# The first step of a fused FFT attention and MLP kernel: a constant matrix loaded and placed later, a load spread over more rows, the last input piece halved

## The chip, the core and the metric

The kernel runs on one core of a Trainium2 chip. A core has a matrix engine (TensorE; the profile calls it PE, and its weight loads PEld), a vector engine (DVE), a scalar engine (ACT), GpSimd (POOL) and a sync engine (SP), and 16 DMA engines. SP and POOL issue the DMAs; what SP issues appears in the profile as queue q1 (hardware), what POOL issues as q0 (software). The metric is the device time of one execution in microseconds (us); less is better.

## The reference

The input x has 8 batches of 3008 tokens with 256 features. Each batch goes through a real FFT along the tokens, a complex linear layer, a soft threshold and an inverse FFT; the result goes through an MLP with a squared ReLU.

```python
X = np.fft.rfft(x, axis=1)
Yr = Xr @ w_r - Xi @ w_i + b_r
Yi = Xr @ w_i + Xi @ w_r + b_i
Y = sign(Y) * max(abs(Y) - 0.01, 0)      # real and imaginary part alike
y = np.fft.irfft(Y, n=3008, axis=1)      # then, with 256 -> 2048 -> 256:
out = (s * max(y @ w_in, 0)**2 + b) @ w_out
```

## The kernel before, in words

3008 tokens are written as 94 x 32 (N1 = 94, N2 = 32), and the FFT is done with matrices. A first matrix A_t (94 x 96) acts on the 94, a forward matrix (the table F_t, and for the imaginary part the tables F_2) acts on the 32, then comes the linear layer, and an inverse matrix T_t and a last matrix C_t bring the result back. The MLP follows: `first_mm` (L1125), a ReLU and a square (L1154 to L1165), and `second_mms` and `seven_mms` (L1241, L1340).

**Two parts.** Batch 0 is done ahead of everything else in `first_batch` (L550). There the framework orders the instructions of each engine from their dependencies; `issue_after(ins)` places what stands under it behind `ins` on the same engine. From there to the end the order is written out by hand (`manual_schedule`, L1494): a table TURNS says which engine takes which copy and when, and each tile of the MLP is interleaved with the FFT work of the next batch. All matrix multiplications go through one helper, so they all carry the line L225; they are told apart by their tiles.

**The first step of batch 0** is the loop in L553 to L589. It has eight groups of four of the 32 columns of x. The x rows come in four tiles of eight columns (`emit_load_x`, L357), each in two DMAs from POOL that also turn f32 into f16: eight pieces of 188 KB, 94 rows each. A group does four matmuls with x and A_t for each half of the features (dc = 0 and 1), each of 96 columns. The results leave PSUM through `evac` (L233), which gives dc = 0 to ACT (L237) and dc = 1 to DVE (L239), into the tile `ut`. Behind each group `keep_awake(5)` adds five matmuls of ones with ones that compute nothing that is used; 40 of them stand ahead of the first group.

**The second stage** starts with `mix` (L602: `ut` times the weights W_t; a bias is added on DVE in L620, the other half is copied by ACT in L617), which needs all 32 columns of `ut`. `fwd_dft` (L630) multiplies by F_t and F_2 and adds a bias through a selector matrix (`sel_t`, a part of the tile `small`), `inv_dft` (L656) multiplies by T_t, and `turn` and `last_dft` bring the data into the form that the MLP reads. There are twelve such steps (ec, u), with u from 0 to 5; step u uses the entries 4u to 4u+3 of the forward matrix.

**The forward matrix** comes for the first 12 of 24 entries in a compact form F_c, which has to be placed into F_t and, with one sign changed, into F_2[0]. `place_f` (L482) does this for a range of entries: one copy on DVE and one on ACT for F_t (L487), and two pairs on DVE for F_2 (L488, L491). The other 12 entries come ready made (F_t[:, H:] and F_2[1]).

**The loads on SP's queue**, in the order in which SP issues them: A_t, the weights w_r and w_i (256 KB each), four bias rows, F_c entries 0 to 3 (64 KB), the selector (32 KB), F_c entries 4 to 11 (128 KB), and then T_t, F_t[:, H:], F_2[1] and T_t[:, H:] with 384 KB each. Two of these are held back by a tiny `memset` on DVE that writes into the target first: F_c entries 4 to 11 until the fourth group has left PSUM (L586), T_t and the rest until the sixth (L580). `place_w` (L478), two casts of the weights on ACT, stands behind the fourth group. Entries 0 to 3 are placed behind the sixth group, entries 4 to 11 behind the first `mix`. When F_t[:, H:] has landed, a copy on POOL (L591) lets the x rows of batch 1 and the MLP weights w_in and w_out be loaded.

Of the kernel before, what the change touches and what calls it, by code (L numbers as in the profile page):

```python
# [15 lines left out]
P = 128  # L16
N1 = 94
# [71 lines left out]
def _tables(n):  # L89

    k1 = np.array([[1 + 2 * p, 2 + 2 * p] for p in range(NPAIR - 1)] + [[0, N1 // 2]])
    n1 = np.arange(N1)
    n2 = np.arange(N2)
    k2 = np.arange(N2)
    first = np.zeros((N1, 96))
    last = np.zeros((96, 96))
    fwd = np.zeros((P, NPAIR, 64))  # L100
    inv = np.zeros((P, NPAIR, 64))
    for p in range(NPAIR):
        for a in range(2):
            c = k1[p, a]
            real = c in (0, N1 // 2)
            th1 = 2 * np.pi * ((n1 * c) % N1) / N1
            kap = 4 * p + 2 * a
            first[:, kap] = np.cos(th1)
            last[kap, :N1] = np.cos(th1)
            if not real:  # L110
                first[:, kap + 1] = -np.sin(th1)
                last[kap + 1, :N1] = -np.sin(th1)
            k = c + N1 * k2
            flip = k > n // 2
            drop = flip if real else np.zeros_like(flip)
            th = 2 * np.pi * (np.outer(n2, k) % n) / n
            sg = np.where(flip, -1.0, 1.0)
            keep = np.where(drop, 0.0, 1.0)
            edge = (k == 0) | (k == n // 2)

            r0 = a * 64
            cr, ci = a * 32, 64 + a * 32
            fwd[r0 : r0 + 32, p, 0:32] = np.cos(th) * keep
            fwd[r0 : r0 + 32, p, 32:64] = -np.sin(th) * sg * keep
            if not real:
                fwd[r0 + 32 : r0 + 64, p, 0:32] = np.sin(th)
                fwd[r0 + 32 : r0 + 64, p, 32:64] = np.cos(th) * sg

            w = np.where(edge, 1.0, 2.0) * keep * VSCALE
            wi = np.where(edge, 0.0, w) * sg  # L130
            inv[cr : cr + 32, p, 0:32] = (np.cos(th) * w).T
            inv[ci : ci + 32, p, 0:32] = (-np.sin(th) * wi).T
            if not real:
                inv[cr : cr + 32, p, 32:64] = (np.sin(th) * w).T
                inv[ci : ci + 32, p, 32:64] = (np.cos(th) * wi).T
    return first, fwd, inv, last
# [13 lines left out]
def kernel(  # L150
# [21 lines left out]
    HW = N2 // 2  # L172

    first, fwd, inv, last = _tables(N)
    last = last / (N * VSCALE)
    A_d = nc.inline_tensor(first.astype(np.float16), name="dft_first").ap()

# [49 lines left out]
    def work(engine, us):  # L227
        load[engine] += us
# [128 lines left out]
    def emit_load_x(b, chunks=range(N2 // XCH)):  # L357
        xv = x[b].rearrange("(n1 n2) d -> n1 (n2 d)", n2=N2)
        for c in chunks:
            if b < 2 and c == N2 // XCH - 1:  # L360
                t = x2pool.tile([P, XCH * D], F16, name="x2", tag="x2")
            else:
                t = xpool.tile([P, XCH * D], F16, name="x16", tag="x16")
            parts = 2 if b == 0 else 1
            w = XCH * D // parts
            for i in range(parts):
                nc.gpsimd.dma_start(
                    out=t[0:N1, i * w : (i + 1) * w],
                    in_=xv[:, c * XCH * D + i * w : c * XCH * D + (i + 1) * w],
                )  # L370
            x16[(b, c)] = t

# [9 lines left out]


    A_t = cpool.tile([P, 96], F16, name="A_t")
    nc.sync.dma_start(out=A_t[0:N1, :], in_=A_d)
    emit_load_x(0)
    W_t = cpool.tile([P, DC, 2, D], F16, name="W_t")
    w_st = []
    for w in (w_r, w_i):
        st = rpool.tile([P, DC, D], F32, name="w_st", tag="rt")  # L390
        nc.sync.dma_start(out=st, in_=w.rearrange("(c p) e -> p c e", p=P))
        w_st.append(st)

    b_g = tpool.tile([P, 2, D], F32, name="b_g", tag="tail")
# [26 lines left out]
    def load_f_c(q):  # L421
        nc.sync.dma_start(out=F_c[:, q].rearrange("p q r k -> p q (r k)"), in_=F_d[:, q])

    load_f_c(slice(0, 4))

    def emit_load_forward():
        load_f_c(slice(4, H))
        nc.sync.dma_start(out=sel_t, in_=S_d)

    def emit_load_inverse():  # L430
        nc.sync.dma_start(out=T_t[:, 0:H], in_=t_d[:, 0:H])
        nc.sync.dma_start(out=F_t[:, H:], in_=f_d)
        nc.sync.dma_start(out=F_2[1], in_=f_2_d)
        t_load = nc.sync.dma_start(out=T_t[:, H:], in_=t_d[:, H:])
        with tc.issue_after(t_load.ins):
            nc.sync.dma_start(out=eye_t, in_=E_d)
            nc.sync.dma_start(out=C_t, in_=C_d)
            for i, bv in enumerate((b_r, b_i)):
                nc.sync.dma_start(out=b_st[:, i], in_=bv.unsqueeze(0).to_broadcast([P, D]))
            nc.sync.dma_start(out=s_bc, in_=moe_s.unsqueeze(0).to_broadcast([P, 1]))  # L440
            nc.sync.dma_start(out=bb_bc, in_=moe_b.unsqueeze(0).to_broadcast([P, 1]))
# [33 lines left out]
    def blocks(t):  # L475
        return t.rearrange("p q (r a k) -> p q r a k", r=2, a=2)
# [2 lines left out]
        for i in range(2):  # L479
            nc.scalar.copy(out=W_t[:, :, i], in_=w_st[i])  # L480

    def place_f(q):  # L482

        for a in range(2):
            r = slice(64 * a, 64 * a + 64)
            copy = nc.scalar.copy if a else nc.vector.tensor_copy
            copy(out=blocks(F_t)[r, q, :, a], in_=F_c[r, q])  # L487
            nc.vector.tensor_scalar_mul(  # L488
                out=blocks(F_2[0])[r, q, 0, a], in0=F_c[r, q, 1], scalar1=-1.0
            )  # L490
            nc.vector.tensor_copy(out=blocks(F_2[0])[r, q, 1, a], in_=F_c[r, q, 0])  # L491


    w_sum = small[:, 2:4]
# [55 lines left out]
    def first_batch():  # L550
        ut = ypool.tile([P, DC, 96, N2], F16, name="ut", tag="yt")
        last_dve = last_act = None
        last_pe = keep_awake(40)  # L553
        for g in range(N2 // 4):
            c, h = divmod(g, 2)
            for dc in range(DC):
                ps = one_bank() if dc else mix_bank()
                with tc.issue_after(last_pe.ins):
                    for j in range(4):
                        lo = (4 * h + j) * D + dc * P  # L560
                        mm = matmul(
                            ps[:, j * 96 : j * 96 + 96],
                            x16[(0, c)][0:N1, lo : lo + P], A_t[0:N1, :],
                            start=True, stop=True,
                        )
                last_pe = mm
                on_dve, on_act = evac(
                    ut[:, dc, :, 4 * g : 4 * g + 4],
                    ps[:, 0:384].rearrange("p (n k) -> p k n", k=96), 384,
                )  # L570
                last_dve = on_dve or last_dve
                last_act = on_act or last_act
            with tc.issue_after(last_pe.ins):
                last_pe = keep_awake(5)
            if h == 0:
                continue
            if c == 2:
                with tc.issue_after(last_dve.ins):
                    for t in (T_t[:, 0:H], F_t[:, H:], F_2[1], T_t[:, H:]):
                        nc.vector.memset(t[0:1, 0, 0:1], 0.0)  # L580
                emit_load_inverse()
                with tc.issue_after(last_dve.ins), tc.issue_after(last_act.ins):
                    place_f(slice(0, 4))
            if c == 1:
                with tc.issue_after(last_dve.ins):
                    nc.vector.memset(F_c[0:1, 4, 0, 0:1], 0.0)  # L586
                emit_load_forward()
                with tc.issue_after(last_act.ins):
                    place_w()  # L589

# [131 lines left out]
        steps = [(ec, u) for ec in range(DC) for u in range(U)]  # L722
        for i in range(2 * U + 2):
            if i < 2 * U:
                left = mix(*steps[i])
            if i == 0:
                with tc.issue_after(left[0].ins), tc.issue_after(left[1].ins):
                    place_f(slice(4, H))
            if 0 <= i - 1 < 2 * U:
                fwd_dft(*steps[i - 1])  # L730
            if 0 <= i - 2 < 2 * U:
                inv_dft(*steps[i - 2])
            k = i - U - 2
            if 0 <= k < 4:
                turn(0, 8 * k)
                turn(0, 8 * k + 4)
            for n in {1: (0, 4), 2: (8, 12), 4: (16, 20, 24, 28)}.get(k, ()):
                last_dft(0, n)
            if i >= 2 * U:
                some(3)  # L740
            if i == 9:

                gate = nc.gpsimd.tensor_copy(out=low[0:1, 0, 0:1], in_=vt[0:1, 1, 0, 0:1])
                with tc.issue_after(gate.ins):
                    make_w_g()
                    make_bounds()
                    sum_w_out()
# [838 lines left out]
```

## Time and profile before

| what | value |
|---|---|
| time, median of 3 runs | 810.1 us (809.83 to 810.39) |
| the profiled execution's own time | 810.04 us |
| its span, first to last instruction | 808.2 us |
| granted TensorE clock over the span | 1.000 |
| chain that ended last, share of PE | 93% |
| first group of the first step starts | 5.39 us |
| first `mix` starts | 14.54 us |
| first matmul of the MLP | 44.85 us |

The page gives the busy time of each engine over the span. The chain that ended last is followed back from the last instruction; its shares say which engine the end waited for. The timeline lists instructions in order of time, with equal neighbours merged: start, busy time, engine, line, what is written and read, and how often. In brackets stands how long the engine stood idle before the first of them and what ended that. A row of waits reads: the waiting engine and what it writes, what it waited for, the total in us, how many times, the longest. A row of the table of stages gives the stretch, its length, then the busy time and count for each of PE, PEld, DVE, ACT and POOL, the granted clock, the share of the DMA engines and GB/s. A row of a DMA queue gives its packets, its MB, and the time of its packets as a share of 16 engines.

### The profile page before, as it was taken

The page shows a single profiled execution, that of the slowest core. Times are in us where ns is not written, and L with a number is a line of the kernel's source. Part 1 is how long each engine was busy: PE and PEld are TensorE (multiplying, and loading weights), DVE is VectorE, ACT ScalarE, POOL GpSimd, SP SyncE. Part 2 cuts the span into 40 slices and gives each one's busy share as a digit, 9 for nine tenths or more (in the row PEclk, how much of TensorE's full clock was granted, in tenths as well). Part 3 has the DMA queues.
Part 4 walks back from the last instruction along what each step waited for, and adds up shares of the span by engine and source line. Part 5 has one row for each costly group of instructions (what it writes and reads, how often), then busy time and mean ns, then how long its engine had stood idle before and what let it go on. Part 6 is the DMA issues. An engine that isn't in the chain of part 4 may idle for free.

```text
span 808.2 us, 22126 instructions
## 1 busy us (share of the span) xinstructions
PE 799.2 (99%) x9006; PEld 613.1 (76%) x9006; DVE 758.9 (94%) x1342; ACT 749.4 (93%) x932; POOL 107.0 (13%) x151
## 2 busy tenths in 40 slices
PE   8999999999999999999999999999999999999998
PEld 7857767777777977788777886778867788777876
DVE  5899999999999999999999999999999999999895
ACT  5989999999999999999999999999999999998984
POOL 4540001110110101111011210012000100000000
PEclk9999999999999999999999999999999999999999
DMA  8983387555774658665686666666556434732213
GB/s 205 190 194 78 95 237 184 102 136 153 208 151 86 153 139 226 145 124 113 169 200 145 135 145 161 152 154 136 137 164 177 108 80 119 183 67 58 62 41 79
DMA packets 120766, 112.89 MB, mean 140 GB/s; under 512 B 9933, under 2 KB 98129, under 8 KB 120665
## 3 DMA queue, kind: packets, MB, share of 16 engines
q1 hardware_dynamic: 102409, 80.55, 36.0%
q0 software_dynamic: 18256, 30.94, 23.2%
q8 instruction: 70, 1.15, 0.6%
q14 instruction: 31, 0.25, 0.1%
HBM read 53.52 MB, written 46.66 MB: 124 GB/s over the span
## 4 chain that ended last, share of the span: by engine, by line
PE 93%; DMA 0%; ACT 0%; DVE 0%; issue 0%; DVEq 0%; ACTq 0%
PE psh L225 40%; PE psa L225 34%; PE psf L225 19%; DMA out_dram<-ost 0%; DVE ost L1278 0%; ACT rt L1154 0%; ACT u L288 0%; DVEq L1278 0%; ACTq L1154 0%
## 5 line engine op out<-in xcount | busy, mean ns | idle before, releaser
L225 PE MATMUL psh<-yt,w_in 128*128 128x512 f16 (+3 forms) x1792 | 444.5, 343 | 0.2 <-ACT rt L1154 0.2
L225 PEld LDWEIGHTS <-gt 128*128 128x128 f16 x4400 | 306.7, 98 | 141.7 <-DVE gt L1325 2.4
L1154 ACT ACTIVATE rt<-psh 128x1024 f32<-128x1024 f32 x339 | 346.9, 1025 | 23.7 <-PE psh L225 21.5
L1163 ACT ACTIVATE gt<-rt 128x1024 f16<-128x1024 f32 x277 | 289.6, 1059 | 3.1 <-DVE rt L1156 0.7
L225 PE MATMUL psa<-w_out_t,gt 128*128 128x128 f16 (+1 forms) x2208 | 199.6, 224 | 0.0
L225 PEld LDWEIGHTS <-w_in 128*128 128x128 f16 x1824 | 152.0, 98 | 15.8 <-issue 1.4
L225 PE MATMUL psa<-T_s,gt 128*128 128x128 f16 x1824 | 144.3, 219 | 0.0
L1317 POOL DMA_DIRECT2D gt<-gt x63 | 54.8, 870 | 650.0 <-DVE s L1325 194.3
L1165 DVE TENSOR_TENSOR gt<-rt 128x1024 f16<-128x1024 f32 x99 | 120.0, 1216 | 2.4 <-ACT rt L1154 2.1
L1390 DVE SCALAR_TENSOR_TENSOR ost<-psa,s_bc,bias_bc 128x256 f32<-128x256 f32 x152 | 72.6, 478 | 6.7 <-PE psa L225 5.7
L1325 DVE TENSOR_TENSOR gt<-gt 128x1024 f16<-128x1024 f16 x109 | 74.4, 682 | 0.7
L1390 DVE SCALAR_TENSOR_TENSOR ost<-psa,s_bc,ost 128x256 f32<-128x256 f32 x129 | 61.6, 477 | 4.0 <-PE psa L225 3.8
L1325 DVE TENSOR_TENSOR gt<-gt,s 128x1024 f16<-128x1024 f16 x86 | 58.8, 684 | 1.4 <-PE psf L225 0.8
L1325 DVE TENSOR_TENSOR s<-gt 128x1024 f16<-128x1024 f16 x86 | 58.7, 683 | 0.5 <-ACT gt L1163 0.2
L880 DVE TENSOR_TENSOR ring<-psf,s 128x512 f16<-128x512 f32 x84 | 57.5, 685 | 1.7 <-PE psf L225 1.0
L225 PEld LDWEIGHTS <-s 128*128 128x128 f16 x688 | 45.4, 98 | 17.6
L225 PE MATMUL psa<-T_s,s 128*128 128x128 f16 x688 | 52.4, 219 | 0.0
L225 PE MATMUL psf<-W_g,xf 128*128 128x256 f16 x336 | 50.4, 273 | 0.0
L1156 DVE TENSOR_SCALAR rt<-psh 128x1024 f32<-128x1024 f32 x37 | 45.0, 1219 | 3.3 <-PE psh L225 1.6
L225 PEld LDWEIGHTS <-xf 128*128 128x128 f16 x504 | 44.7, 98 | 3.3
L225 PE MATMUL psf<-x,A_t 94*96 94x512 f16 x103 | 39.3, 382 | 0.3 <-DVE u L288 0.2
L225 PE MATMUL psf<-C_t,vs 96*128 96x96 f16 x484 | 38.3, 205 | 0.3 <-DVE u L288 0.3
(116 smaller groups left out, 836.6 us busy)
## 6 DMA issues: line engine op xcount, KB each, us to landing
out_dram<-ost SPq DMA_DIRECT2D x74, 256.0 KB
gt<-gt POOLq DMA_DIRECT2D x63, 256.0 KB, 4.0
ud<-u SPq DMA_DIRECT2D x56, 192.0 KB
us<-ud SPq DMA_DIRECT2D x28, 384.0 KB
vd<-v SPq DMA_DIRECT2D x42, 256.0 KB
vs<-vd SPq DMA_DIRECT2D x28, 384.0 KB
x<-in_x_dram POOLq DMA_DIRECT2D x56, 188.0 KB, 5.6
ring<-ring SPq DMA_DIRECT2D x120, 64.0 KB
```

The lines of the kernel that those rows point to most:

```text
L225: return nc.tensor.matmul(out, lhs, rhs, **how)
L880: lambda e: nc.vector.tensor_tensor(out=ring[0][:, i % 4], in0=ps, in1=hold[i // 2][:, i % 2].unsqueeze(1).to_broadcast([P, 2, D]), op=ALU ...
L1154: nc.scalar.activation(out=rt, in_=ps, func=AF.Relu)
L1156: nc.vector.tensor_scalar(out=rt, in0=ps, scalar1=0.0, scalar2=None, op0=ALU.max)
L1163: nc.scalar.activation(out=gt, in_=rr, func=AF.Square)
L1165: nc.vector.tensor_tensor(out=gt, in0=rr, in1=rr, op=ALU.mult)
L1317: nc.gpsimd.dma_start(out=a12, in_=a11, accum_op=ALU.add)
L1325: nc.vector.tensor_tensor(out=out, in0=a, in1=b, op=op)
L1390: ins = nc.vector.scalar_tensor_tensor(out=out(), in0=hold[of], scalar=s_bc[0:size], in1=other(), op0=ALU.mult, op1=ALU.add,)
```

## The change

- A_t is loaded with 96 rows in place of 94 (two rows of zeros), and SP issues that load behind w_r, not first.
- The last tile of x comes in three DMAs, of 4, 2 and 2 columns, and the last group of the first step is split in two groups of two columns.
- F_c entries 0 to 3 are held back until the second group has left PSUM; entries 4 to 11 and the selector until the sixth, ahead of T_t on the queue. `place_w` moves from the fourth group to the second.
- Placing is split: entries 0 to 3 of F_t behind the group that starts at column 16, the first half of their F_2 behind the next, the second half behind the last group. For entries 4 to 11, F_2 comes ahead of F_t.
- The filling matmuls behind a group are eight in place of five, and three ahead of the last half group. Every `mix` is put behind the last of them on PE.
- dc = 0 is given to ACT and dc = 1 to DVE outright, with the planner's account of both engines' work kept up.

```diff
+    first = np.concatenate([first, np.zeros((96 - N1, 96))])
...
+            ends = [0, XCH] if b else [0, 4, 6, 8] if c == N2 // XCH - 1 else [0, 4, 8]
+            for lo, hi in zip(ends, ends[1:]):
+                at = c * XCH * D
                 nc.gpsimd.dma_start(
+                    out=t[0:N1, lo * D : hi * D], in_=xv[:, at + lo * D : at + hi * D]
                 )
...
-    nc.sync.dma_start(out=A_t[0:N1, :], in_=A_d)
...
+        if not w_st:
+            nc.sync.dma_start(out=A_t[0:96, :], in_=A_d)
...
-    load_f_c(slice(0, 4))
-
-    def emit_load_forward():
+    def emit_load_inverse():
         load_f_c(slice(4, H))
         nc.sync.dma_start(out=sel_t, in_=S_d)
-
-    def emit_load_inverse():
         nc.sync.dma_start(out=T_t[:, 0:H], in_=t_d[:, 0:H])
...
-    def place_f(q):
-
+    def place_f_t(q):
         for a in range(2):
             r = slice(64 * a, 64 * a + 64)
             copy = nc.scalar.copy if a else nc.vector.tensor_copy
             copy(out=blocks(F_t)[r, q, :, a], in_=F_c[r, q])
...
+    def place_f_2(q, a):
+        r = slice(64 * a, 64 * a + 64)
+        nc.vector.tensor_scalar_mul(
+            out=blocks(F_2[0])[r, q, 0, a], in0=F_c[r, q, 1], scalar1=-1.0
+        )
+        nc.vector.tensor_copy(out=blocks(F_2[0])[r, q, 1, a], in_=F_c[r, q, 0])
...
+        groups = [(lo, 4) for lo in range(0, N2 - 4, 4)] + [(N2 - 4, 2), (N2 - 2, 2)]
...
+                if dc:
+                    last_dve = nc.vector.tensor_copy(out=dst, in_=src)
+                    work("dve", over["dve"] + k / 10)
+                else:
+                    last_act = nc.scalar.copy(out=dst, in_=src)
+                    work("act", over["act"] + k / 12.5)
             with tc.issue_after(last_pe.ins):
-                last_pe = keep_awake(5)
-            if h == 0:
+                last_pe = keep_awake(3 if n == N2 - 4 else 8)
+            with tc.issue_after(last_dve.ins), tc.issue_after(last_act.ins):
+                if n == 16:
+                    place_f_t(slice(0, 4))
+                if n in (20, N2 - 2):
+                    place_f_2(slice(0, 4), int(n > 20))
+            if at == 0:
                 continue
             if c == 2:
                 with tc.issue_after(last_dve.ins):
-                    for t in (T_t[:, 0:H], F_t[:, H:], F_2[1], T_t[:, H:]):
-                        nc.vector.memset(t[0:1, 0, 0:1], 0.0)
+                    for t in (F_c[:, 4], sel_t, T_t[:, 0:H], F_t[:, H:], F_2[1], T_t[:, H:]):
+                        nc.vector.memset(t[0:1, 0:1, 0:1] if len(t.shape) > 2 else t[0:1, 0:1], 0.0)
                 emit_load_inverse()
-                with tc.issue_after(last_dve.ins), tc.issue_after(last_act.ins):
-                    place_f(slice(0, 4))
-            if c == 1:
+            if c == 0:
                 with tc.issue_after(last_dve.ins):
-                    nc.vector.memset(F_c[0:1, 4, 0, 0:1], 0.0)
-                emit_load_forward()
+                    nc.vector.memset(F_c[0:1, 0, 0, 0:1], 0.0)
+                load_f_c(slice(0, 4))
                 with tc.issue_after(last_act.ins):
                     place_w()
...
             if i < 2 * U:
-                left = mix(*steps[i])
+                with tc.issue_after(last_pe.ins):
+                    left = mix(*steps[i])
             if i == 0:
                 with tc.issue_after(left[0].ins), tc.issue_after(left[1].ins):
-                    place_f(slice(4, H))
+                    for a in range(2):
+                        place_f_2(slice(4, H), a)
+                    place_f_t(slice(4, H))
```

## The prediction

> **What bounds the kernel now.** I read the page first, then the table of stages over the first 50 us, the waits and the timeline of the first step, and the DMA queues there. The page's engine row and its chain:
>
> ```profile
> PE 799.2 (99%) x9006; PEld 613.1 (76%) x9006; DVE 758.9 (94%) x1342; ACT 749.4 (93%) x932; POOL 107.0 (13%) x151
> ...
> PE 93%; DMA 0%; ACT 0%; DVE 0%; issue 0%; DVEq 0%; ACTq 0%
> ```
>
> TensorE sets the end. The change touches nothing behind the second stage, where the order is written out by hand; so it is worth what it shifts the start of the later work, if that shift is kept. Where can TensorE start earlier? The stages (length, then PE, PEld, DVE, ACT, POOL busy):
>
> ```profile
> 5.39:14.54 9.15, 6.93 (x106) 5.46 (x105) 4.99 (x18) 5.16 (x11) 2.08 (x4) 1.00 0.98 190
> 14.54:20.00 5.46, 5.27 (x57) 4.53 (x58) 4.58 (x12) 3.94 (x7) 2.38 (x6) 1.00 0.96 298
> 20.00:35.00 15.00, 15.00 (x204) 13.71 (x202) 12.90 (x22) 13.95 (x27) 9.08 (x12) 1.00 1.00 188
> 35.00:50.00 15.00, 13.48 (x125) 8.63 (x123) 14.87 (x25) 12.65 (x24) 10.44 (x12) 1.00 1.09 202
> ```
>
> In the first step the DMA engines are busy for 0.98 of the time and no compute engine is full. In 14.54 to 35 TensorE is full, in 35 to 50 DVE (14.87 of 15.00). The waits from 5.3 to 15 say what the first step waits for:
>
> ```profile
> PEld L225 <- DMA x<-in_x_dram: 3.6, 8, 1.0
> PE psm L225 <- DMA x<-in_x_dram: 2.0, 6, 0.8
> ...
> PEld L225 <- ACT ut L237: 0.3, 1, 0.3
> ```
>
> All eight groups wait for their piece of x, and `mix` waits for the last copy out of PSUM. The end of the step in the timeline (start, busy):
>
> ```profile
> 13.62 0.34 PE L225 MATMUL psm<-A_t,x 94*128 94x96 f16 x4 [0.17 <-DMA x<-in_x_dram]
> 13.80 0.33 PE L225 MATMUL psf<-A_t,x 94*128 94x96 f16 x4
> 13.97 0.45 PE L225 MATMUL psa<-ones 128*128 128x128 f16 x5
> ...
> 14.00 0.48 ACT L237 CAST ut<-psm 128x384 f16<-128x384 f32 x1 [0.49 <-PE psm L225]
> ...
> 14.54 1.92 PE L225 MATMUL psm<-W_t,ut 128*128 128x256 f16 x16
> ```
>
> So the step's end is the landing of the last piece (13.57 us, by its semaphore in the trace) plus 0.97 us. Two things can move: the landing, and this tail.
>
> **The landing.** The DMA engines are full from about 3.3 us until the last piece, so a load taken out of that time gives its share back. (a) The selector and F_c. From 7 to 10.5 us q1 carries F_c entries 0 to 3 (64 KB) and the selector (32 KB), 290 packets with markers, and q0 moves 0.62 MB of x, 0.177 MB per us; from 10.5 to 12.3, with 4 packets on q1, 0.35 MB, 0.194 per us. Over 3.5 us that is 0.06 MB or 0.31 us. The change takes out the selector alone (F_c 0 to 3 moves from 7 us to about 9.5, still before the end): a third by bytes, half by packets, 0.10 to 0.15 us; I take 0.1. F_c entries 4 to 11 mostly came after the bulk of x (125 packets on q1 in 12.3 to 13.4): nothing to at most 0.1. (b) w_r is issued first: SP's A_t issue at 0.73 no longer stands ahead of that at 1.11, so w_r starts 0.38 us earlier, on DMA engines that carry nothing else then. In 3.3 to 4.3 us, when x has begun, q1 still had 87 packets, 22% of 16 engines, 0.22 us. That much leaves the time of x: 0.2 us, between 0 and 0.38. w_i keeps its issue at 1.71. A_t lands behind w_r, whose last landing was 4.38, now about 4.0; x needs it at 5.39: hidden by 1.3 us. (c) Halving the last piece adds a POOL issue of 0.53 us; POOL had issued its eight pieces by 5.5 us, and the fill of F_2 behind it (7.72, 1.0 us) is read after 15 us: hidden. Sum: the last x lands **0.3 us** earlier, between 0 and 0.6.
>
> **The tail.** The last group has 2 matmuls per half, not 4: at 0.18 us for 4 that saves 0.09. ACT's copy has 192 columns: 0.48 us for 384 and 0.58 for 512 (L617) give 0.78 ns a column, 0.33 us, which saves 0.15. Together 0.24; `mix` starts 0.73 us behind the landing. The eight fillers behind that group fit: 0.18 us of matmuls and 8 x 0.055 = 0.44 end at landing + 0.67, by the spacing of the five fillers. I take **0.2 us**, between 0.1 and 0.25. DVE's half saves more, 0.36, and `mix` needs it later. The three extra fillers elsewhere (0.17 us) fit in TensorE's waits for weights of x, 0.28 to 0.99 us; if x came faster than a group's 0.36 + 0.44 us they would hold it up, and it comes every 0.9 to 1.1. The granted clock is 1.00 with and without them.
>
> **What else is moved, at nothing.** F_c entries 0 to 3 are issued behind DVE's copy of group two (7.54 + 0.56), at about 8.2; the gated load of F_c 4 to 11 took from 11.16 to its last landing at 14.76, 3.6 us, T_t from 13.15 to 15.89, 2.7. So it is there at 11.3 to 12.1, and the placing behind group five starts at about 11.6. At worst DVE and ACT stand for 0.5 us, with the copies of groups six and seven queued behind; DVE idles 0.35 to 0.5 us in each group, which takes most of it back: 0 to 0.2 us at `mix`. The placing itself (DVE 12.77 to 13.5, ACT 0.40) is spread over three groups, the last third behind DVE's last copy, where DVE was idle for 0.78. `place_w` (ACT, 1.14 us) moves to about 7.9, where ACT idles 1.14; w_i had landed at 6.04. Two more memsets are 0.06 each. For entries 4 to 11 the same seven copies run in another order, ending alike. SP's queue behind the sixth group gets F_c (0.32) and the selector (0.43) in front: T_t, F_t, F_2[1] leave about 0.5 us later, or, x being 0.3 earlier, about 0.2. F_2[1] landed at 19.43 and is read at 21.49; T_t[:, H:] landed at 20.40 and is read at 23.85; the gate of POOL (17.30) moves alike, and what comes behind it, w_out above all, feeds a matmul at 53.5 through sums that POOL ends at 47.9. All have a us or more to spare even with readers 0.5 earlier. The planner's account differs by 0.02 us in its difference of ACT and DVE; followed through its rule, every later copy keeps its engine.
>
> **Sum.** 0.3 + 0.2 = 0.5 us, which the full TensorE of 14.54 to 35 and the full DVE of 35 to 50, both started earlier, hand on. The profiled execution took 810.04 (span 808.2), next to the median of 810.1: **809.5 us**. A difference of 0.2%, 1.6 us, is about the least that a measurement of this kernel can tell from no change; most cases lie inside.
>
> **Rivals.** *Late engines.* Of the 16 counts of the last piece 14 come by 13.02, the others at 13.17 and 13.57; the third piece shows the same (7.85, 8.16, 8.56). A_t's 94 packets run as two series, and its semaphore has 14 counts at once and the last two at 2.50 and 2.52: two engines carry it all. If these two are the late ones and 96 rows spread the load, the last x comes up to 0.55 earlier still: 809.0; with every term at its far end 808.5. Against it: A_t's packets end at 2.44 and w_r's begin at 2.30 to 2.54, so little was delayed, and x of batch 1 has late engines too (27.75 against 26.9). The four bias rows, on one engine each, stay. The Trainium skill, page "DMA: Bandwidth & Descriptors", section "Latency and other measured facts", says that DMA engines 7 and 15 are usually slower when POOL issues; by that rule the lag stays and the sum is 809.5, by the two-engine reading 809.0. No view here names an engine.
>
> *The shift is swallowed.* x keeps its pace, the placing takes the tail's gain, or DVE's stage absorbs it: 810.0. Against it: nothing else in that stage waits for a fixed time. That the split does not take (the two small pieces landing together) ends here as well.
>
> *The selector comes late: slower.* It now leaves behind F_c 4 to 11 at about 12.6 us and is read in the first `fwd_dft`, which would be at 16.0. With 2.7 us of flight it is there at 15.8. With 3.6, and F_c's placing on DVE (0.9 us) ahead of the next bias additions, TensorE stands for 0.5 to 0.9 us: the gain is gone. From about 3.5 us of flight on it decides; at 5.6, what T_t[:, H:] took (14.82 to 20.40, behind other loads), TensorE stands for about 2.2: 811.7. Between, 810.8. For it: it waits with five loads behind it; against it: only 160 KB go first, when x has just ended.
>
> **Chances.** Forecast 0.48; late engines 0.18; swallowed 0.16; late selector 0.14; something else 0.04. Half of the late engines, with the other terms at their ends, and 0.03 reach 1.6 us faster: 0.12. The far third of the late selector and 0.04 reach slower: 0.09. Range: 808.5 to 811.0.
>
> **What would show it.** Right: the last x group at about 13.3, `mix` 0.7 us behind it, no wait of TensorE for `small` or F_c before 20 us, the first MLP matmul near 44.3, the rest shifted alike. Wrong: the last group before 12.9 (late engines), PEld waiting for a DMA at 15 to 18 us (selector), or an MLP start that has not moved (swallowed).

## The result, and the profile after

The changed kernel takes **813.39 us** (median of 5 runs, 813.35 to 815.44) against 810.39 us for the kernel before in the same session (5 runs, 809.83 to 810.92). The ratio is 1.0042, 95% interval 1.003 to 1.0053: slower by 0.3 to 0.5%. The forecast was 809.5 with a range up to 811.0.

The profiled execution of the changed kernel took 815.44 us (span 813.7), 2 us above its median. A second profile of the same kernel, taken later, lies below the median (812.81, span 811.0); where a size matters, both are given. In the changed kernel every matmul has the line L226, the copies out of PSUM in the first step are L573 (ACT) and L570 (DVE), and the placing of F_t is L483. The engine row and the chain of the page after:

```profile
PE 802.6 (99%) x9033; PEld 616.7 (76%) x9033; DVE 759.4 (93%) x1345; ACT 749.7 (92%) x933; POOL 107.5 (13%) x152
...
PE 91%; DMA 2%; DVE 1%; ACT 0%; issue 0%; DVEq 0%; ACTq 0%
```

TensorE still sets the end, with 3.4 us more of busy time than before (799.2). The second profile has 800.3 with the same 9033 matmuls, 27 of them added fillers; most of the rest is the clock of this execution, as the stages show (columns as in the table of stages before):

```profile
8.30:11.70 3.40, 3.40 (x39) 3.40 (x40) 1.12 (x3) 1.97 (x4) 1.97 (x3) 0.50 1.10 196
...
14.80:16.60 1.80, 0.05 (x2) 0.00 (x0) 0.73 (x4) 0.72 (x2) 0.00 (x0) 1.00 0.01 1
...
17.90:22.00 4.10, 4.10 (x29) 3.19 (x27) 2.69 (x10) 1.79 (x3) 0.00 (x0) 0.58 0.86 282
22.00:40.00 18.00, 18.00 (x236) 16.21 (x235) 15.42 (x25) 16.53 (x30) 11.59 (x17) 1.00 0.95 199
```

From 14.80 to 16.60 TensorE does next to nothing, and the DMA engines are idle too (0.01): the last packet of x and F_c ends at 14.97, and the last counts of their semaphores come at 15.30 (x) and 15.77 (F_c entries 0 to 3). The row of 17.90 has a granted clock of 0.58: 29 matmuls in 4.1 us, where the kernel before did 57 in 5.46. The waits up to 22 us name what came late:

```profile
ACT F_t L483 <- DMA F_c<-dft_fwd: 2.8, 1, 2.8
DVE F_t L483 <- DMA F_c<-dft_fwd: 2.5, 1, 2.5
...
PE psf L226 <- DVE ut L570: 2.0, 2, 1.8
```

Both copying engines stand for F_c entries 0 to 3, and TensorE stands for DVE. The timeline of the end of the step shows how one leads to the other:

```profile
15.85 0.40 ACT L483 COPY F_t<-F_c 64x256 f16<-64x256 f16 x1 [2.77 <-DMA F_c<-dft_fwd]
15.87 0.22 DVE L483 COPY F_t<-F_c 64x256 f16<-64x256 f16 x1 [2.54 <-DMA F_c<-dft_fwd]
16.01 0.54 DVE L570 CAST ut<-psf 128x384 f16<-128x384 f32 x1
...
16.61 0.24 PE L226 MATMUL psf<-A_t,x 94*128 94x96 f16 x2 [1.75 <-DVE ut L570]
...
16.70 0.06 DVE L587 MEMSET F_c<- 1x1 f16 x1
...
16.75 0.56 DVE L570 CAST ut<-psf 128x384 f16<-128x384 f32 x1
```

The order of each engine is fixed. Behind the placing stand the copies of groups six and seven (L570, L573); until they have run, TensorE has no PSUM bank for the next group, so it stands for 1.75 us. Behind the same copy on DVE stand the six memsets that release the later loads: the first at 16.70, where the kernel before had the first of its four at 12.72:

```profile
12.72 0.06 DVE L580 MEMSET T_t<- 1x1 f16 x1
```

So T_t, F_t[:, H:] and the gate of POOL come late as well (22.18 us, 17.30 before). `mix` starts at 17.90 (14.54 before; 16.79 in the second profile), and the first matmul of the MLP at 49.60 (44.85 before; 46.95).

### The profile page after: what moved, and what is told of

It reads as the page before. It is cut to its first block, busy times and chain, and to the rows that moved or that the text cites. A ratio compares the mean times of both kernels' runs of the same rounds, so it can differ in the third digit from the quotient of the medians.

```text
span 813.7 us, 22186 instructions
## 1 busy us (share of the span) xinstructions
PE 802.6 (99%) x9033; PEld 616.7 (76%) x9033; DVE 759.4 (93%) x1345; ACT 749.7 (92%) x933; POOL 107.5 (13%) x152
## 4 chain that ended last, share of the span: by engine, by line
PE 91%; DMA 2%; DVE 1%; ACT 0%; issue 0%; DVEq 0%; ACTq 0%
PE psh L226 39%; PE psa L226 33%; PE psf L226 19%; DMA gt<-gt 1%; DVE gt L1173 1%; DMA out_dram<-ost 0%; DVE u L289 0%; DVE ost L1286 0%; ACT rt L1162 0%; DVE vs L289 0%; DVE ost L1398 0%; DVEq L1286 0%; ACTq L1162 0%
## 5 line engine op out<-in xcount | busy, mean ns | idle before, releaser
L226 PE MATMUL psh<-yt,w_in 128*128 128x512 f16 (+3 forms) x1792 | 444.5, 343 | 0.4 <-ACT rt L1162 0.4
L226 PEld LDWEIGHTS <-gt 128*128 128x128 f16 x4400 | 306.7, 98 | 142.1 <-DVE gt L1333 2.4
L1171 ACT ACTIVATE gt<-rt 128x1024 f16<-128x1024 f32 x277 | 289.6, 1059 | 3.3 <-DVE rt L1164 0.8
L226 PE MATMUL psa<-w_out_t,gt 128*128 128x128 f16 (+1 forms) x2208 | 199.7, 224 | 0.3 <-DMA gt<-gt 0.3
L226 PEld LDWEIGHTS <-w_in 128*128 128x128 f16 x1824 | 152.0, 98 | 16.0 <-issue 1.7
L226 PE MATMUL psa<-T_s,gt 128*128 128x128 f16 x1824 | 144.2, 219 | 0.0
L226 PEld LDWEIGHTS <-s 128*128 128x128 f16 x688 | 45.4, 98 | 17.6
L226 PE MATMUL psa<-T_s,s 128*128 128x128 f16 x688 | 52.4, 219 | 0.0
L226 PE MATMUL psf<-W_g,xf 128*128 128x256 f16 x336 | 50.4, 273 | 0.0
L226 PEld LDWEIGHTS <-xf 128*128 128x128 f16 x504 | 44.8, 98 | 3.3
L226 PE MATMUL psf<-x,A_t 94*96 94x512 f16 x103 | 39.3, 381 | 0.3 <-DVE u L289 0.2
L226 PE MATMUL psf<-C_t,vs 96*128 96x96 f16 x484 | 38.2, 205 | 0.3 <-DVE u L289 0.3
```

Of the source, the lines that this page charges most:

```text
L226: return nc.tensor.matmul(out, lhs, rhs, **how)
L1171: nc.scalar.activation(out=gt, in_=rr, func=AF.Square)
```

## The experiments

Each kernel was timed beside the kernel before on the same chip; 810.31 to 810.45 us was its median in every session. Intervals are 95%. There were five sessions, each on another chip, and some of the differences below are between kernels of two sessions; this is said where it is so.

### The hold of entries 0 to 3, and their placing

**The changed kernel once more**, without an edit. 

> The changed kernel as it is, for a second profile beside the edits. In the first one F_c entries 0 to 3 landed at 15.77 us, ACT and DVE stood 2.8 and 2.5 us for them, mix began at 17.90 and the granted clock was 0.50 in two stretches. Theory (late F_c): the wait of ACT and DVE for F_c comes back, over 1 us, and the time is 813 to 815. Rival (first pieces): the first x group again starts over 1 us later than 5.39 and the clock falls before 12 us, whatever F_c does. Rival (chance): F_c lands before 13 us, mix begins before 15 and the time is near 810.

813.65 us (812.55 to 818.69, 6 runs), ratio 1.0047 [1.0025, 1.0068]. Its profile shows the same wait (ACT 3.1 us, DVE 2.9; F_c 0 to 3 issued at 8.86, landed at 14.66) with a granted clock of 1.00 throughout. So the wait belongs to the kernel, the half clock to some of its executions. The median hardly rests on the clock: the executions of the changed kernel with 0.999 or 1.000 over the span took 812.81, 813.35 and 813.39 us in the two timings, those with less 812.55 to 818.69.

**Entries 0 to 3 loaded from the start.**

```diff
+    load_f_c(slice(0, 4))
...
-                with tc.issue_after(last_dve.ins):
-                    nc.vector.memset(F_c[0:1, 0, 0, 0:1], 0.0)
-                load_f_c(slice(0, 4))
```

> The changed kernel with one part undone: F_c entries 0 to 3 are loaded from the start, without the memset that held them; everything else stays, the point of placing too. Late F_c: no wait for F_c on ACT or DVE, mix begins by 15 us and the time falls by 2 to 4 us to 809.5 to 811. First pieces: the first group stays late and the clock falls before 12 us, the time stays at 812 or more. Last half piece: mix still begins after 16 us because the ninth x transfer lands after 15.

811.89 us, ratio 1.0018 [1.0005, 1.0032]. The load stands where the kernel before has it; beside the second timing of the changed kernel 1.8 us of the loss are gone, and with them the wait for F_c (landed at 10.79). The intervals of the two kernels still touch.

**The hold kept, all placing of entries 0 to 3 behind the last group.**

```diff
-                if n == 16:
+                if n == N2 - 2:
                     place_f_t(slice(0, 4))
-                if n in (20, N2 - 2):
-                    place_f_2(slice(0, 4), int(n > 20))
+                    for a in range(2):
+                        place_f_2(slice(0, 4), a)
```

> The changed kernel with the load of F_c entries 0 to 3 held as in the change, but all of their placing behind the last group, so that no copy out of PSUM stands behind it on ACT or DVE. Late F_c with the queue as its price: the groups no longer stand, mix begins by 15 to 15.6, fwd_dft waits for F_c instead, at most 0.5 to 1 us; the time falls by 1.5 to 3 us. If the lateness itself is the price and not the queue, the time stays within 0.5 us of the changed kernel. First pieces: no change either.

811.33 us, ratio 1.0007 [0.9998, 1.0017]. The load is as late as ever (issued at 9.52, landed at 14.43), but nothing stands behind it any more:

```profile
14.05 0.79 ACT L573 CAST ut<-psm 128x192 f16<-128x192 f32 x2 [0.23 <-PE psm L226]
...
14.86 0.40 ACT L483 COPY F_t<-F_c 64x256 f16<-64x256 f16 x1
...
14.89 0.94 PE L226 MATMUL psm<-W_t,ut 128*128 128x256 f16 x7
```

The copies of the last two half groups come first, the placing at 14.86 waits for nothing, and `mix` starts at 14.89, 0.73 us behind the last landing of x (14.16). The interval lies below that of the changed kernel. So it is not the hold alone that costs, but the placing ahead of copies that TensorE needs.

**The kernel before with the hold alone.**

```diff
-    load_f_c(slice(0, 4))
...
+            if c == 0:
+                with tc.issue_after(last_dve.ins):
+                    nc.vector.memset(F_c[0:1, 0, 0, 0:1], 0.0)
+                load_f_c(slice(0, 4))
```

> The kernel before with one part of the change alone: F_c entries 0 to 3 held back until the second group has left PSUM. Their placing stays behind the sixth group, with all four copies. Late F_c: it is issued near 8.2 us and lands near 13, ACT and DVE stand 0.3 to 1.5 us for it behind group six, mix begins 0.3 to 1.5 us later and the time rises by as much, to 810.7 to 812. If only the new point of placing (a group earlier) makes the load late, the time stays within 0.3 us of the kernel before.

811.02 us, ratio 1.001 [1.0001, 1.0019]. The waits of this kernel:

```profile
ACT F_t L485 <- DMA F_c<-dft_fwd: 1.6, 1, 1.6
...
DVE F_t L485 <- DMA F_c<-dft_fwd: 1.3, 1, 1.3
```

Here the placing stands one group later (behind group six), the wait is 1.3 to 1.6 us, `mix` is 0.62 late (15.16) and the median 0.67: the same mechanism, with about half the wait.

### The order of the weights and the first matrix

**The changed kernel with the first matrix ahead of w_r again.** The edit moves the line `nc.sync.dma_start(out=A_t[0:96, :], in_=A_d)` back to the front of SP's queue; the third and fourth of this group make the same edit.

> The changed kernel with A_t (96 rows) issued ahead of w_r again. First pieces: x begins within 0.3 us of 5.39, the clock does not fall before 12 us, and the time falls by 1 us or more. Late F_c: the wait for F_c stays over 1 us and the time stays within 0.7 us of the changed kernel.

813.97 us, ratio 1.0045 [1.003, 1.006]. The first group starts at 5.28 again (6.56 in the changed kernel, 5.39 before), but the wait for F_c swallows that (2.9 and 2.7 us).

**The kernel before with 96 rows of A_t**, nothing else (`out=A_t[0:96, :]` and two rows of zeros).

> The kernel before with one part of the change alone: A_t loaded with 96 rows, still first on SP's queue. Late engines rival of the prediction: the 15th and 16th count of each x piece no longer trail by 0.15 and 0.55 us, the last x comes up to 0.5 us earlier, 809.8 to 810.0 where the kernel before is at 810.4. Otherwise the trailing stays and the time is within 0.15 us of the kernel before.

810.51 us, ratio 1.0005 [0.9996, 1.0014]: no difference can be seen.

**The kernel before with 96 rows and w_r ahead of A_t.**

> The kernel before with the weights ahead of the first matrix (in 96 rows), nothing else. If the order of the two loads decides when x begins and the end of x stays with the queues: the first group at 6.0 to 6.8 in place of 5.39, last x and mix as before, 810.2 to 810.7. If the late first piece carries through to the last x: mix up to 0.5 us later, 810.7 to 811.0. If the prediction's gain is there: last x 0.1 to 0.2 earlier, 810.1 to 810.3.

811.26 us, ratio 1.0011 [1.0002, 1.002]: 0.75 us above the run with 96 rows alone (another session).

**The kernel with all placing last, and A_t first.** 

> The kernel with all placing of entries 0 to 3 behind the last group (811.33) and the first matrix ahead of the weights again. If the order of these two loads makes the rest of the loss: 0.7 to 0.9 us less, 810.4 to 810.7. If it is the additions of POOL beside the first squares, or the held load itself: 811.1 to 811.5 as before the edit.

810.77 us, ratio 1.0004 [0.9996, 1.0013]: 0.56 us less than with w_r first (another session).

**The changed kernel without the hold, and A_t first.** 

> The changed kernel without the hold (entries 0 to 3 loaded from the start, 811.89) and with the first matrix ahead of the weights again. If the order of the loads costs 0.8 us wherever it stands: 811.0 to 811.3. If the placing behind groups five, six and nine, or the late loads behind group six, make that version slow: 811.6 to 812.1, as before the edit.

810.83 us, ratio 1.0003 [0.9994, 1.0012]: 1.06 us less (another session). Three pairs of kernels that differ in this order alone give 0.56, 0.75 and 1.06 us, all in one direction, but each pair is of two sessions and the two intervals of each overlap; the fourth pair, the changed kernel with its wait for F_c, gives 0.3 us the other way. That w_r first costs is likely, not shown. The clock alone does not make it: among executions with 0.999 or 1.000 over the span the medians of the three pairs still differ by 0.4, 0.8 and 1.1 us.

By what way the order acts is not settled. The traces show one difference: w_r lands at 3.53 to 3.72 in the eight profiles with w_r first (3.88 to 5.68 with A_t first), but w_i, the load behind it, at 7.02 to 9.19, where it lands at 6.04 to 6.63 in ten of the twelve with A_t first (8.32 and 8.33 in the others). So the weights reach further into the time of x, not less far.

### The pieces of x, the split group and the later loads

**The last x tile in three transfers and the group split, without the rest.** With the split come three fillers between the two halves, every `mix` behind the last filler, and the engines given outright (these edits are not shown below).

```diff
+            ends = [0, XCH] if b else [0, 4, 6, 8] if c == N2 // XCH - 1 else [0, 4, 8]
...
+        groups = [(lo, 4) for lo in range(0, N2 - 4, 4)] + [(N2 - 4, 2), (N2 - 2, 2)]
```

> The kernel before with the last x tile in three transfers (4, 2 and 2 n2) and the last group cut in two with the fillers between; no held load, the first matrix ahead as before. If the split of the last x is a small gain, as the prediction had it: the last piece lands at 13.4 to 13.6, mix 0.73 us behind it at 14.2 to 14.3, 810.0 to 810.2. If a ninth x transfer costs time in itself (in the kernels that have it, it landed at 13.82 to 15.38, where the eighth of before lands at 13.57): it lands near 14.2 or later, mix at 14.9 or later, 810.6 to 811.2.

810.42 us, ratio 1.0 [0.9991, 1.0008]. The last piece lands at 13.45, `mix` starts at 14.40 (13.57 and 14.54 before). So the way from the landing to `mix` is 0.95 us (0.97 before), not the 0.73 of the kernel with all placing last: here DVE still places entries 0 to 3 ahead of these copies, TensorE stands 0.28 us for it (until 14.04), and `mix` stands behind five fillers that start at 14.12.

**The group split alone**, x in eight pieces. 

> The kernel before with only the last group of the forward stage cut in two (2 and 2 n2, the fillers between), the x transfers as before in eight pieces. Both halves then wait for the same landing near 13.57. If the smaller copies give back what the prediction had: mix 0.7 to 0.8 us behind the landing in place of 0.97, 810.1 to 810.3. If three more fillers and the second pair of copies behind the same landing cost as much as they save: 810.4 to 810.8.

810.49 us, ratio 1.0003 [0.9994, 1.0011]. Its `mix` starts at 14.23, 0.31 us earlier, and the first MLP matmul at 44.33, 0.52 earlier; the first matmul with w_out is 0.65 late (55.95 for 55.30). The earlier `mix` comes from an earlier last piece in this execution (13.16 for 13.57): from the landing to `mix` it is 1.07 us, 0.10 longer than before. What comes late behind it is taken up in the next group.

**The kernel with all placing last, x in eight pieces.** 

> The kernel with all placing behind the last group, and the last x tile in two transfers as before, groups still cut in two. If the ninth x transfer is what makes the last x late (14.16 in that kernel, 13.57 in the kernel before): the last x lands at 13.4 to 13.7, mix at 14.2 to 14.5, 810.7 to 811.1, with what remains from the additions of POOL beside the first squares (0.8 us in that kernel's run). If the late last x comes from the held load's place in the queues or the weights' order: it lands at 14.1 again and the time is 811.2 to 811.5.

811.86 us, ratio 1.0014 [1.0005, 1.0023], no better than with nine (another session). Its times lie in two bunches, five at 810.75 to 811.0 and six at 811.86 to 813.21. The bunches go with the clock: it is 0.999 or 1.000 over the span in the five, 0.998 in five of the six; the profile (810.82) shows the last x at 14.41, held by one of 16 counts (the one before came at 13.12). The run tells nothing against the half pieces and nothing for them.

**The kernel with all placing last, F_c 4 to 11 and the selector loaded where the kernel before has them.** 

> The changed kernel with all placing of entries 0 to 3 behind the last group, and the loads of F_c entries 4 to 11 and of the selector at their places of before (behind group four, and ungated), so that T_t, F_t and F_2 leave SP's queue 0.8 us earlier. Theory (POOL beside DVE, because its gate comes late): the gate of POOL comes at 17.3 to 18, POOL's sums end before 48.5, the squares shorten, and the time is 0.3 to 0.8 us below 811.3. Rival: the selector's earlier load costs x its pace and gives back 0.1 to 0.2; if the gate does not matter, 811.3 to 811.5.

811.15 us, ratio 1.001 [1.0001, 1.0019]; 811.33 without the edit (another session). That the later place of these two loads costs can't be seen.

### The additions of POOL beside the first squares

**The kernel with all placing last, and four of POOL's seven additions of the parts of w_out left out** (the bias lacks those parts). 

> The changed kernel with all placing of entries 0 to 3 behind the last group, and four of POOL's seven additions for the sums of w_out left out (L520), so the bias that goes into the output is not the full one. With the additions in, this kernel began the MLP 0.15 us later than the kernel before but was 0.8 us behind at 56 us: DVE's first squares took 1.82 and 2.71 us in place of 1.21 and 2.35 while POOL still added. Theory (POOL beside DVE): with POOL done before 47 us the first squares take 1.2 and 2.35 us, and the time falls by 0.4 to 0.8 us against 811.3, to 810.5 to 810.9. Rival (squares wait for something else): they stay long, the time stays at 811.3.

811.10 us, ratio 1.0009 [1.0, 1.0018]; 811.33 with all additions (another session). The median says little, but the profile shows the first two squares at 1.21 us each, with 1.82 and 1.57 when all additions are done.

What happens there shows best in the group split (start, busy time; L521 is POOL's addition, L1170 the square on DVE):

```profile
47.12 1.17 POOL L521 TENSOR_TENSOR acc<-acc,w_out_t 128x512 f32<-128x512 f32 x1
47.40 1.99 DVE L1170 TENSOR_TENSOR gt<-rt 128x1024 f16<-128x1024 f32 x1
48.37 2.02 POOL L521 TENSOR_TENSOR small<-acc,w_out_t 128x512 f16<-128x512 f32 x1
49.91 2.71 DVE L1170 TENSOR_TENSOR gt<-rt 128x1024 f16<-128x1024 f32 x2
```

and in the kernel before (L1165 is the square):

```profile
46.68 1.16 POOL L521 TENSOR_TENSOR small<-acc,w_out_t 128x512 f16<-128x512 f32 x1
47.73 1.21 DVE L1165 TENSOR_TENSOR gt<-rt 128x1024 f16<-128x1024 f32 x1
49.58 2.35 DVE L1165 TENSOR_TENSOR gt<-rt 128x1024 f16<-128x1024 f32 x2
```

Elsewhere a square takes 1.21 us and an addition 1.16. In the group split the two take turns: the square that starts at 47.40 lasts until the addition's end (48.29) plus 1.10; the next addition lasts until the square's end (49.39) plus 1.00; the second square (1.57 of the 2.71) until the addition's end (50.39) plus 1.09. The Trainium skill, page "SBUF — State Buffer", section "SBUF: two separate sides", states that DVE, when it reads two inputs from SBUF, and GpSimd hold a shared pair of ports exclusively, so that the later one waits for the whole of the other's instruction; the trace agrees within 0.16 us three times. In the kernel before, POOL's last addition ends at 47.84 and the first square starts at 47.73: they just miss each other. Over the profiles:

| kernel | `mix` | first square | POOL's sums end | extra of the first two squares |
|---|---|---|---|---|
| before | 14.54 | 47.73 | 47.84 | 0 |
| changed | 17.90 | 52.49 | 53.01 | 0.39 |
| changed, second profile | 16.79 | 49.84 | 52.20 | 0.50 |
| all placing last | 14.89 | 47.88 | 50.71 | 0.97 |
| w_r first | 14.95 | 48.15 | 48.81 | 0.53 |
| group split | 14.23 | 47.40 | 50.40 | 1.14 |
| all placing last, A_t first | 14.78 | 47.78 | 47.62 | 0 |

The starts of the squares follow `mix`; the end of the sums follows the gate of POOL (18.29 in the group split, 17.30 before). An earlier `mix` with a later gate makes the two overlap.

**The group split, and the kernel before, each with four additions left out.** 

> The kernel before with the last group cut in two, and four of POOL's seven additions of w_out's parts left out (the bias lacks those parts). If the additions beside the first squares swallow what the group split gains: the gain shows against the same kernel without the split, 0.3 to 0.5 us less than it. If the split gains nothing in itself: the same time as that kernel.

> The kernel before with four of POOL's seven additions left out (the bias lacks those parts): the measure for the run above. If the additions of POOL cost nothing where they end with the first square (47.84 and 47.73 us in the trace of before): 810.2 to 810.5. If they cost in most of its executions: 809.6 to 810.1.

809.83 us against 810.53 (ratios 0.9992 [0.9983, 1.0] and 1.0004 [0.9992, 1.0015]), the split 0.7 below; with all additions 810.49 and 810.41 to 810.45. But the two intervals overlap, the two profiled executions took 810.56 and 810.14, the other way round, and much of the 0.7 goes with the clock: it was below 0.999 over the span in 4 of 11 executions with the split and in 9 of 12 without, and among the others the medians are 809.65 (7) and 809.83 (3). That the squares can be held up is shown by their durations; that the split has a gain to give is not shown, and the 1.07 us from landing to `mix` speak against it.

**The sums kept whole and started earlier**: the first two loads of w_out ahead of w_in, with the group split and without.

```diff
-        for dc in range(DC):
-            nc.gpsimd.dma_start(out=w_in_t[dc], in_=moe_w_in[dc * P : (dc + 1) * P, :])
         for q in (slice(q, q + 4) for q in range(0, MC, 4)):
+            if q.start == 8:
+                for dc in range(DC):
+                    nc.gpsimd.dma_start(out=w_in_t[dc], in_=moe_w_in[dc * P : (dc + 1) * P, :])
```

> The kernel before with the last group cut in two, and the first two of w_out's four loads ahead of the two of w_in. If POOL's sums then start up to 2 us earlier and end ahead of the second square, the split's gain is kept: 809.8 to 810.2. If the sums start no earlier, or the other loads come too late for it (w_in is read at 44.3): 810.4 to 811.

> The kernel before with the first two of w_out's four loads ahead of the two of w_in, nothing else: the measure for the run above. POOL's sums end at 45.8 to 46.5 in place of 47.84, ahead of the first square at 47.73, which they hardly meet now: 810.2 to 810.5. If w_in comes too late: 810.6 or more.

809.99 us (ratio 0.9997 [0.9988, 1.0006]) with the split, 810.15 (1.0001 [0.9993, 1.001]) without; the kernel before in that session 810.31. The profile with the split (L522 is the addition, L1171 the square):

```profile
46.12 1.16 POOL L522 TENSOR_TENSOR small<-acc,w_out_t 128x512 f16<-128x512 f32 x1
47.77 1.21 DVE L1171 TENSOR_TENSOR gt<-rt 128x1024 f16<-128x1024 f32 x1
```

The sums end ahead of the first square and the square is short again. This is the lowest median of the kernels that compute everything, but its interval includes no change: it isn't shown to be better.

## Why the prediction was wrong, point by point

**The step that failed** is "F_c entries 0 to 3 ... held", priced "at nothing: 0 to 0.2 us at `mix`". It took the flight from two loads that ran when x had nearly ended (3.6 and 2.7 us from the end of their issues, 3.9 and 3.1 from the start). The trace of before had a nearer row, the same 64 KB in the time of x, with its last count at 9.32, 5.9 us from the start of its issue:

```profile
3.45 0.36 SPq L422 DMA_DIRECT2D F_c<-dft_fwd  x1
```

The held load has its last count at 15.77, 6.1 us from its issue:

```profile
9.69 0.36 SPq L423 DMA_DIRECT2D F_c<-dft_fwd  x1
```

It took 5.8 us in the second profile and 4.9 to 6.3 in the seven other kernels that hold it. In the changed kernel's first profile 15 of its 16 counts are there at 14.58, 4.9 us from the issue, and the last comes 1.2 us later, as with x (below); in the second they are 5.4 and 0.4 us. With the prediction's own issue at 8.2 and 5.9 us it lands at 14.1, 2.5 us behind the 11.6 at which placing starts; ACT and DVE were measured to stand for 2.8 and 2.5, in a kernel where all of this ran about 1.5 us later. The prediction did name what is queued behind, the copies of groups six and seven; its mistake was 0.5 us where 2.5 belonged, so that DVE's idle time could not take it back. Undoing the hold took 1.5 to 1.8 us off, moving the placing behind the last group 2.1 to 2.3 (the ends are the two timings of the changed kernel).

**w_r first** was to bring the last x 0.2 us earlier, between 0 and 0.38. No run shows that gain, and the sign is likely the other: x's first group starts at 5.50 to 6.79 in the kernels with w_r first (5.20 in one), at 5.28 to 5.87 with A_t first, and three pairs of kernels give 0.56 to 1.06 us slower. A_t is not what is late: behind w_r it lands at 3.70 to 3.88. w_r does land earlier, as reckoned, but w_i lands later than in ten of the twelve kernels with A_t first. The held load, which waits for the second group, was issued at 8.53 to 9.69 in the six profiles with w_r first, and at 8.07 to 8.57 with A_t first in three; the prediction reckoned 8.2.

**The last x** was to land at about 13.3. In the changed kernel it lands at 15.30 (13.82 in the second profile), and in the eight other kernels with nine pieces at 13.45 to 15.38. With eight pieces it lies between 13.16 and 14.41. In the changed kernel 15 of its 16 counts are there at 14.07. From 14.00 to 14.25 the only packet under way is one of 16 KB on the instruction queue (0.97 us from 13.30 on), and behind its end the last packets of x and F_c run one after another until 14.97; no packet names its engine, so that one engine carried them all is inferred. Terms of 0.1 and 0.2 us can't be told in such a spread.

**The tail** was right where the placing is out of the way: 0.73 us from the landing to `mix` forecast, 0.72 to 0.79 measured in six of the seven kernels with nine pieces in which no copy waits for F_c. It is 0.95 in the seventh, with the pieces and the split alone, where DVE's placing stays just ahead of the last copies, and 1.07 in three kernels with the split and eight pieces (1.45 in a fourth). In the changed kernel itself it is 2.6 us (3.0 in the second profile), because the copies stand behind the placing.

**"All have a us or more to spare"** was wrong for the gate of POOL. The prediction followed it to the data's reader (a matmul at 53.5) and found room; it did not look at what runs beside POOL's sums. They held DVE's first squares up for 0.1 to 1.1 us in eleven profiles; what this makes of the whole time no run separates from the spread. The two loads put in front on SP's queue were also worth more than the 0.5 us reckoned: their two terms, 0.32 and 0.43, add up to 0.75, and with all placing last F_c leaves at 13.20, T_t at 14.11.

**The rivals.** *Late engines* fell: 96 rows change nothing (1.0005 [0.9996, 1.0014]). *The selector comes late* had the right sign and the wrong load: a late load with work queued behind its reader, but no wait of TensorE for `small` is among the waits, and loading it early changed 0.2 us, within the intervals. *Swallowed* fits the split and the pieces alone (ratios 1.0003 and 1.0), but no run shows that there was a gain to swallow.

**The half clock** was not foreseen. In the changed kernel's profile the granted clock is 0.50 from 8.30 to 11.71 and from 18.54 to 21.96. The second follows the 1.75 us without work; it stretches the way from `mix` to the first `inv_dft` from 4.62 to 6.01 us. The second profile has none. It is not the change's alone: six other profiles show a half clock between 7.3 and 14.2 us, two of them of kernels whose first step is that of before, and by the executions at full clock above it is not what makes the 3 us. The Trainium skill, page "TensorE: Matmul & The Clock Gate", section "Part 1: The HAM clock gate", puts the fall to half rate behind an idle window of about 3.4 us, in windows that run freely. The length agrees (3.41 us); but in the window ahead of 18.54 TensorE was idle for no more than 1.5 us at a stretch, so less than a whole idle window was enough here. Nor does the longest stretch decide: the second profile has one of 1.45 us in the window from 11.72 to 15.13 and keeps the full clock. What goes with the fall is how long TensorE was busy in the window: 1.39 and 1.67 us of 3.41 ahead of the two falls here, 1.97 and 1.94 in two windows of the second profile that kept the clock. Over the first 25 us of all profiles, a window at full clock with 1.86 us or less was always followed by the half clock (seven times), one with 2.02 or more never, and between 1.90 and 1.99 there are both.

**What stays open.** With the hold or the placing undone and A_t first, 810.8 us are left, 0.4 above before, within the intervals; these two kernels keep the other parts of the change (fillers, `place_w`, the order of entries 4 to 11), so those cost nothing that can be seen together. Whether and why w_r first costs is open. POOL's gate opens anywhere from 17.3 to 18.6 in kernels that load F_t alike, 0.1 us behind F_t's landing. A part of that spread is in the traces: in three kernels with the split SP issues F_t earlier than before (12.80 to 13.13 for 13.24), but the issue lasts 0.98 to 1.30 us and F_t lands at 18.03 to 18.16 (17.17 before). In the group split:

```profile
12.80 1.30 SPq L432 DMA_DIRECT2D F_t<-fwd_rest  x1
```

In the kernel before:

```profile
13.24 0.63 SPq L432 DMA_DIRECT2D F_t<-fwd_rest  x1
```

Why the issue lasts so long was not found.

## What to carry to other kernels

Price a held load by the flight of the same load at the same time of the kernel, not by loads that fly when the queues are free; and put the work that reads it behind everything that the matrix engine waits for, since an engine in order makes every later copy wait too. A gain at the start can be taken back downstream: look in the trace of before for a pair of instructions that just miss each other (here 47.84 and 47.73 us), and ask whether both move. And read a gain of some tenths of a us in one profile against its own landing times and clock before it is given to the edit: the earlier `mix` of the group split came with an earlier piece of x.

## What the runs showed of the hardware

- A square on DVE (two inputs from SBUF) and an addition on POOL shut each other out: a square of 1.21 us took up to 1.99, an addition of 1.16 us 2.02.
- One packet of 16 KB on the instruction queue, of 0.88 to 0.97 us, starts between 11.6 and 13.7 us in every profile. In the changed kernel the last counts of x and of F_c came 1.2 us behind the others, their packets behind the end of that one; a last count of x that is 0.9 to 1.3 us late is in six other profiles too.
- A 64 KB load from SP among the x transfers took 4.9 to 7.3 us from issue to landing in the twenty profiles, held or not.
- A window of 3.41 us in which TensorE was busy for 1.39 to 1.86 us was followed by the half clock for the next, seven times of seven; one with 2.02 us or more never was, from the full clock and within the first 25 us.
